# First batch of a gated-MLP attention kernel: f32 products and transpositions on TensorE in place of split halves and DMA transpositions

## Chip, core and metric

The kernel runs on one core of one Trainium2 chip. The metric is the device time of one launch in microseconds (us); before the change it is the median of three runs. PE is TensorE, DVE VectorE, ACT ScalarE, POOL GpSimd, SP the engine that issues all the DMAs here.

## What is computed

Eight batches of eight heads of causal attention with an added decay, and then a gated MLP per batch. Sequence 576, head width 64, model width 512, MLP width 1024.

```python
scores = scale * np.matmul(q, k.transpose(0, 1, 3, 2))
bias = -(cum[:, :, :, None] - cum[:, :, None, :])      # cum = cumsum(max(s, 0))
scores = np.where(causal, -1000000000.0, scores + np.minimum(bias, 0.0))
scores = scores - np.max(scores, axis=-1, keepdims=True)
attn = np.exp(scores)
attn = attn / (np.sum(attn, axis=-1, keepdims=True) + 1e-09)
x = np.matmul(attn, v)                                  # heads side by side: 576 x 512
h = np.maximum(x @ w_in, 0.0)
u, v = (h[..., :d_ff // 2], h[..., d_ff // 2:])
v_n = (v - mu) / np.sqrt(var + 1e-06)
v_s = np.einsum('ts,bsd->btd', w_spatial, v_n) + b_spatial[None, :, None]
out = (u * v_s) @ w_out
```

## The kernel before

Work is cut into 32 **pairs** of heads (four pairs make a batch) and eight MLPs. Where f32 accuracy is wanted, most operands are kept as two f16 halves, a high and a low one, and a product is two or three f16 matmuls; the three weights are split in this way once, at the start.

A pair p goes through these steps (names as the planner has them):

- `sc`: scores, in seven PSUM groups (`BANKS`). From pair 3 on (`NNAT = 3`) they come from two f16 matmuls (L463), whose operands ACT rounds (`h`, L413), POOL subtracts (`l`, L406) and four DMAs move into place. Pairs 0 to 2 take f32 q and k as they are loaded and one f32 matmul (L460), with the decay rows copied in by `nsel` (L304) and `ncum` (L308). A f32 matmul leaves two records in the trace.
- `red` (L469, DVE): mask and row maximum. `exp` (L487, ACT): exponential and row sum. `sum` (L492, L493, L497, DVE): the inverse of the sums.
- `hi` (L513, ACT) and `lo` (L515, DVE): the normalised weights as high and low halves, four instructions each per head, and one each for the two heads' last 64 rows (`thi`, `tlo`).
- `turn`, `tturn` (L522): three DMA transpositions per pair, issued by SP.
- `av` (L620, L627, PE): weights times V in three f16 products; V's halves come from `vh` (L585, ACT) and `vl` (L587, DVE), for two pairs at a time. `xh`, `xl` (L636, L640) split the result for the MLP.

An MLP runs `gate` (L670), `up` (L764), the spatial product `sp` (L779, L781, L782) and `dn` (L808) on PE, with ACT, DVE and POOL between them. The weights' conversion at the start is `wb`, `wq`, `wd`, `wh`, `wl` (L340 to L349, L320, L321) for each of twelve blocks, DVE in the main.

The order on every engine is made when the kernel is built: `Plan.order` walks through all steps with a guessed duration for each and takes, on each free engine, the ready step with the lowest place. The places come from the table of numbers `X`. On the chip each engine then works through its own list strictly in that order, and waits where an operand or a buffer isn't ready. PSUM has three banks each in `psS` and `psM` for scores and MLP products, one for `av` and one for the last rows.

Of the kernel before, what the change touches and what calls it, by code (L numbers as in the profile page):

```python
# [17 lines left out]
SV = 64.0  # L18
# [115 lines left out]
X = {"load": -5.2, "prep": -2.2, "vf": -0.5, "vc": 1.5, "red": 0.0, "exp": 0.092, "sum": -0.172, "hi": -0.219, "lo": -0.36, "turn": 0.06, "tsum": 0.528, "thi": 0.133, "tlo": 0.08, "tturn": 0.09, "av": 3.72, "av3": 5.635, "xh": 0.358, "xl": -0.701, "m0": 10.3, "span": 8.0, "mb0": -0.073, "mb1": 0.0, "n1": -25.0, "n2": 2.0, "l3": 0.5, "p3": 4.805, "vf0": 0.688, "vc0": 1.4, "vf1": 4.402, "vc1": 6.4, "fv": 1.483, "fvd": 1.2, "cv": 7.171, "cvd": 0.531, "fu": 4.5, "fud": 1.0, "cu": 9.0, "cud": 0.5, "wo": 10.6, "wod": 1.1, "sp": 11.0, "spd": 0.4, "sp4": 10.635, "bias": 0.2, "hv": 0.0, "bn": 0.01, "nm": 0.03, "vh": 0.04, "vl": 0.05, "uc": -0.671, "gm": 0.0, "gh": 0.01, "gl": 0.02, "oc": -0.113, "out": 0.01, "sc": 0.333, "sc0": 0.0, "up0": 0.0, "sp0": 0.0, "dn0": 0.0}  # L134


def mm(*cols):
    return sum(0.4167 * c + 3 for c in cols)
# [11 lines left out]
def attn_gated_mlp(ctx, tc, qkT, v, s, w_in, w_spT, b_sp, w_out, outT):  # L150
# [20 lines left out]
    NNAT = 3  # L171
# [25 lines left out]
    mhalf = cp.tile([P, 1], F32, name="mhalf")  # L197
    cc = cp.tile([NH, 3, S], F16, name="cc")
# [18 lines left out]
    def masks4():  # L217
# [5 lines left out]
        nc.gpsimd.memset(mhalf, -0.5)  # L223

    add("mb", POOL, 1700, -19, masks)
    add("mb4", POOL, 1200, -18, masks4)
# [61 lines left out]
    add("bp", POOL, 6000, X["bias"] + .1, lambda: bias_rows(1), need=["bf"])  # L288
# [4 lines left out]
    ntag = (("g1", "g2", 1, ["g1", "g2"]), ("xt1", "xt2", 2, ["xt"]), ("xt1", "xt2", 2, ["xt"]))  # L293
# [9 lines left out]
    def native_sel(p):  # L303
        [nc.vector.tensor_copy, nc.scalar.copy, nc.scalar.copy][p](  # L304
            raws[p, "q"][0:NH], sel[:, 2 * p:2 * p + 2].unsqueeze(2).to_broadcast([NH, 2, S]))

    def native_cum(p, j):
        [nc.vector.tensor_copy, nc.vector.tensor_copy, nc.scalar.copy][p](raws[p, "k"][0:NH, j], cst["cum"])  # L308

    for p in range(NNAT):  # L310
        at = (-27.0, X["n1"], X["n2"])[p]
        add(("nk", p), SYNC, 650, at, lambda p=p: native_load(p, "k"), take=ntag[p][3], move=(0, 1070))
        add(("nq", p), SYNC, 650, at + .1, lambda p=p: native_load(p, "q"), need=[("nk", p)], move=(0, 1070))
        add(("nsel", p), (DVE, ACT, ACT)[p], (700, 1150, 1150)[p], at + .2, lambda p=p: native_sel(p), need=[("nq", p)])
        for j in range(2):
            add(("ncum", p, j), (DVE, DVE, ACT)[p], (400, 400, 650)[p], at + .3 + .1 * j,
                lambda p=p, j=j: native_cum(p, j), need=[("nk", p), "cum"])
# [73 lines left out]
    BLK = (2, 0, 3, 6)  # L391
    pts = {}
# [32 lines left out]
    def attend(p):  # L425
# [98 lines left out]

        for b, (j, ics) in enumerate(BANKS):
# [45 lines left out]
    def values(hb):  # L571
        i = hb % 2

        def fetch():
            b, x = divmod(hb, 2)
            cols = slice(4 * D * x, 4 * D * x + 4 * D)
            raw = wk.tile([P, NC5, 4 * D], F32, tag="vraw", bufs=1, name=f"vraw{hb}")
# [5 lines left out]
        old = [("av", 2 * hb - 3)] if hb > 1 else []  # L583
        add(("vf", hb), SYNC, 1000, a0, fetch, take=["vraw"], move=(0, 1660))
# [13 lines left out]
    def output(p):  # L598
# [4 lines left out]
        def products():  # L603
            ph, pt4 = [pts.pop((p, j)) for j in range(2)], pts.pop((p, None))
            if pr == 0:
                xt[b] = (wk.tile([P, KC, S], F16, tag="xt1", bufs=2, name=f"xt1_{b}"),
                         wk.tile([P, KC, S], F16, tag="xt2", bufs=2, name=f"xt2_{b}"))
                avt[b] = psT.tile([P, 4, TAIL], F32, tag="T", name=f"avt{b}")
            av = avs[p] = psV.tile([P, 512], F32, tag="V", name=f"av{p}")
            for jc in range(NFULL):  # L610
                for n, (off, V) in enumerate(((0, V1), (0, V2), (10, V1))):
                    for q0 in ((max(jc, 1), 0) if jc == 0 else (jc,)):
                        for j in range(2):
# [4 lines left out]
                            else:  # L618
                                rhs, dst = ph[j][:, off + BLK[0]], av[o, 0:P]
                            nc.tensor.matmul(dst, V[i][:, jc, h + j], rhs, start=jc == n == 0 and q0 > 0,  # L620
                                             stop=jc == 3 and n == 2)
            t = avt[b][:, pr]
            for jc in range(NC5):
                for n, (off, V) in enumerate(((0, V1), (0, V2), (5, V1))):
# [267 lines left out]
```

## Time and profile before

| | |
|---|---|
| median of three runs | 677.1 us (675.7 to 677.91) |
| the profiled execution | 675.81 us, of which the span in the trace is 674.0 us |
| busy over the span | PE 593.3, DVE 570.7, ACT 508.8, POOL 137.0 us |
| mean granted PE clock | 0.959 of 2.4 GHz |

Busy PE means that a matmul was in flight. A share of the span is an average over a start in which PE has little to do and a long rest in which it has no pause, so the stretches are shown apart below. The granted clock is a share of full speed: 1.00 is 2.4 GHz, and a stretch between 0.5 and 1.0 was at 1.2 GHz for a part of it.

### The profile page before, as it was taken

What the parts mean: (1) busy time and instruction counts of PE and PEld (TensorE: products, weight loads), DVE (VectorE), ACT (ScalarE), POOL (GpSimd) and SP (SyncE); (2) the same over time, 40 slices, a digit from 0 to 9 for tenths busy, and PEclk for the clock granted to TensorE, in tenths of its full rate; (3) what the DMA queues carried; (4) which work ended last, traced back from release to release, by engine and by line L of the source; (5) the groups of instructions that cost most, each with busy time, mean ns of one, the idle gap of its engine ahead of it and who ended that gap; (6) DMA issues with size and microseconds to landing.
All of it is one profiled execution on the core that took longest, in us unless ns stands there. A gap on an engine that the chain in (4) does not pass through costs nothing. (4 is left out here: it accounts for less than half of the span.)

```text
span 674.0 us, 15717 instructions
## 1 busy us (share of the span) xinstructions
PE 593.3 (88%) x5696; PEld 408.7 (61%) x5696; DVE 570.7 (85%) x1544; ACT 508.8 (75%) x1319; POOL 137.0 (20%) x188
## 2 busy tenths in 40 slices
PE   2556446979998999999998999899999999999997
PEld 1232322757746775677656775677566765777675
DVE  6999999999799898989898989989888989892630
ACT  4868678796878788788968897879869887874422
POOL 9720221110312112311132021211231111000200
PEclk9886757989999999999999999999999999999999
DMA  8999999978997999879986999598967987564001
GB/s 249 290 216 237 142 205 222 211 195 160 172 240 151 178 216 241 158 148 239 203 195 147 220 186 236 136 202 194 244 164 129 217 183 130 92 117 131 1 13 70
DMA packets 245347, 119.28 MB, mean 177 GB/s; under 512 B 213864, under 2 KB 227350, under 8 KB 245271
## 3 DMA queue, kind: packets, MB, share of 16 engines
q1 hardware_dynamic: 245271, 118.30, 81.2%
q8 instruction: 44, 0.72, 0.4%
q14 instruction: 32, 0.26, 0.1%
HBM read 37.48 MB, written 9.66 MB: 70 GB/s over the span
## 5 line engine op out<-in xcount | busy, mean ns | idle before, releaser
L487 ACT ACTIVATE p<-psS,mx 128x128 f32<-128x128 f32 (+3 forms) x256 | 133.2, 526 | 38.3 <-DVE mx L469 37.5
L406 POOL TENSOR_TENSOR QB<-raw,KA 128x288 f16<-128x288 f32 x116 | 89.6, 802 | 299.8 <-ACT KA L413 299.7
L469 DVE CUSTOM_DVE_ANT_0 psS<-psS,mb 128x128 f32<-128x128 f32 (+3 forms) x288 | 134.5, 475 | 8.2 <-PE psS L463 2.8
L513 ACT ACTIVATE pb<-p,sm 128x384 f16<-128x384 f32 (+3 forms) x256 | 123.5, 552 | 22.3 <-issue 11.6
L515 DVE SCALAR_TENSOR_TENSOR pb<-p,sm,pb 128x384 f16<-128x384 f32 (+3 forms) x256 | 129.9, 556 | 5.2 <-ACT pb L513 3.9
L463 PE MATMUL psS<-KA,QA 128*128 128x128 f16 (+1 forms) x348 | 83.0, 313 | 32.6 <-ACT p L487 23.9
L764 PE MATMUL ups<-xt,win 128*128 128x288 f16 x768 | 102.4, 286 | 7.3 <-ACT u L769 7.2
L779 PE MATMUL sps<-ws,vn 128*128 128x288 f16 x768 | 105.5, 287 | 0.0
L808 PE MATMUL ops<-g,wo 128*128 128x288 f16 x768 | 101.5, 286 | 0.7 <-ACT ob L815 0.7
L670 PE MATMUL vps<-win,xt 128*128 128x512 f16 (+1 forms) x576 | 99.0, 348 | 0.1
L764 PEld LDWEIGHTS <-win 128*128 128x128 f16 x768 | 73.9, 98 | 33.0 <-issue 11.2
L808 PEld LDWEIGHTS <-wo 128*128 128x128 f16 x768 | 74.5, 98 | 25.0 <-issue 2.7
L463 PE MATMUL psS<-KB,QB 128*128 128x128 f16 (+1 forms) x348 | 89.3, 308 | 0.0
L779 PEld LDWEIGHTS <-vn 128*128 128x128 f16 x768 | 74.3, 98 | 24.2 <-issue 2.1
L670 PEld LDWEIGHTS <-xt 128*128 128x128 f16 (+1 forms) x576 | 47.8, 103 | 48.8 <-issue 7.1
L620 PE MATMUL av<-pT,V 128*64 128x128 f16 (+2 forms) x960 | 63.1, 285 | 8.0 <-DMA pT<-pb 5.5
L696 POOL TENSOR_TENSOR rs<-rs,mhalf 128x1 f32<-128x1 f32 x40 | 24.8, 619 | 199.4 <-DVE rs L692 175.0
L620 PEld LDWEIGHTS <-V 128*64 128x64 f16 x960 | 49.2, 115 | 26.4 <-issue 14.7
L463 PEld LDWEIGHTS <-QA 128*128 128x128 f16 x348 | 30.2, 102 | 37.2 <-issue 29.9
L487 ACT ACTIVATION_READ_ACCUMULATOR p<-psS,mx 128x1 f32 x256 | 51.5, 201 | 0.0
L460 PE MATMUL psS<-kraw,qraw 128*128 128x128 f32 (+5 forms) x72 | 23.5, 553 | 27.4 <-ACT p L487 14.0
L469 DVE DVE_READ_ACCUMULATOR2_ANT mx<- 128x1 f32 x320 | 45.6, 142 | 0.0
(80 smaller groups left out, 791.2 us busy)
## 6 DMA issues: line engine op xcount, KB each, us to landing
raw<-in_qkT_dram SPq DMA_DIRECT2D x29, 576.0 KB
out_dram<-ob SPq DMA_DIRECT2D x32, 288.0 KB
vraw<-in_v_dram SPq DMA_DIRECT2D x16, 512.0 KB
QA<-KA SPq DMA_DIRECT2D x29, 144.0 KB
KB<-KA SPq DMA_DIRECT2D x29, 144.0 KB
KB<-QB SPq DMA_DIRECT2D x29, 144.0 KB
QB<-KA SPq DMA_DIRECT2D x29, 144.0 KB
wst<-in_w_in_dram SPq DMA_DIRECT2D x8, 512.0 KB
```

What stands on the lines that cost most here:

```text
L406: nc.gpsimd.tensor_tensor(out=QB[i][:, j, cs], in0=raws[p][:, j, cs], in1=KA[i][:, j, cs], op=ALU.subtract)
L463: nc.tensor.matmul(ps[m, c0:c0 + w], U[i][:, g, q0:q0 + n], T[i][:, g, k0:k0 + w], start=st, stop=not st)
L469: nc.vector.tensor_tensor_reduce(out=ps[:, c0:c0 + w], in0=ps[:, c0:c0 + w], in1=mask, op0=ALU.add, op1=ALU.min, scale=-0.125, scalar=mx[: ...
L487: nc.scalar.activation(dst, ps[:, c0:c0 + w], AF.Exp, bias=mx[:, mcol:mcol + 1], scale=-1.0, accum_out=sm[:, col:col + 1])
L513: nc.scalar.activation(dst[:, off:off + w], src, AF.Copy, bias=0.0, scale=sc)
L515: nc.vector.scalar_tensor_tensor(out=dst[:, n + off:n + off + w], in0=src, scalar=sc, in1=dst[:, off:off + w], op0=ALU.mult, op1=ALU.subtract)
L620: nc.tensor.matmul(dst, V[i][:, jc, h + j], rhs, start=jc == n == 0 and q0 > 0, stop=jc == 3 and n == 2)
L670: nc.tensor.matmul(ps[m, 0:w], xx[:, c, t * P:t * P + (m.stop - m.start)], ww[:, c, NF + g * w:NF + g * w + w], start=c == n == 0, stop=c ...
L696: nc.gpsimd.tensor_tensor(out=rs, in0=rs, in1=mhalf, op=ALU.pow)
L764: nc.tensor.matmul(ps[:, 0:TH], ww[:, c, fs], xx[:, c, ts], start=n == 0, stop=n == 3 * KC - 1)
L779: nc.tensor.matmul(ps[:, 0:TH], vv[:, c, fs], ww[:, c, ts], start=n == 0, stop=False)
L808: nc.tensor.matmul(ps[:, 0:TH], ww[:, f, ms], gg[:, f, ts], start=n == 0, stop=n == 3 * FC - 1)
```

## The change

For the first batch (pairs 0 to 3, `NNV = 4`) three things change.

- Pair 3's scores are f32 products too (`NNAT = 4`): its `h`, `l` and four DMA moves go, `nsel` and `ncum` on ACT come.
- The weights aren't split and no DMA transposes them. POOL multiplies an identity matrix that holds 64 on its diagonal (`eye`) by the inverse sums, which gives a diagonal matrix per block of 128 rows (`dg`, 512 and 640 columns a pair). PE multiplies each of the 25 blocks of 128x128 exponentials of a pair by its diagonal in f32 (`tp`), which transposes and normalises it in one product; ACT copies the result from PSUM (`te`, eight copies a pair, f32).
- `av` takes these and V as it was loaded, one f32 product in place of three f16 ones, so `vh` and `vl` of the first two loads go.

The diagonals and the second load of V use the buffers `pb` that held the halves. All numbers in `X` are others too, so the order on every engine differs, in the later batches as well. At the start SP issues two blocks of `w_in` and a third k ahead of the first q, and DVE does the first block's `wb` ahead of `nsel` of pair 0.

```diff
-    NNAT = 3
+    NNAT = 4
+    NNV = 4
...
+        nc.gpsimd.memset(eye, 0.0)
+        nc.gpsimd.affine_select(out=eye, in_=eye, pattern=[[-1, P]], compare_op=ALU.not_equal, fill=SV, base=0,
+                                channel_multiplier=1)
...
+        def diagonals(j):
+            if j == 0:
+                cell["dg"] = wk.tile([P, 10, P], F32, tag="pb", bufs=room["pb"], name=f"dg{p}")
...
+            n = 4 + j
+            eng.tensor_tensor(out=cell["dg"][:, 4 * j:4 * j + n], in0=eye.unsqueeze(1).to_broadcast([P, n, P]),
+                              in1=cell["sm"][:, 4 * j:4 * j + n].unsqueeze(2).to_broadcast([P, n, P]), op=ALU.mult)
+
+        def transpose(j, k):
...
+            for x, n in enumerate(TB[j][k]):
...
+                nc.tensor.matmul(ps[:, P * x:P * x + P], src, cell["dg"][:, col], start=True, stop=True)
+
+        def keep(j, k):
...
+            src = cell["tp", j, k][:, 0:P * len(blocks)].rearrange("p (n q) -> p n q", q=P)
+            if EV[j][k] is ACT:
+                nc.scalar.copy(dst, src)
...
+            if p < NNV:
+                dg = DG[p]
+                add(("dg", p, j), dg, {POOL: 1450 + 350 * j, DVE: 700 + 130 * j}[dg], at + X["dg"], lambda j=j: diagonals(j),
+                    need=[("sum", p, j), "mb4"], take=["pb"] if j == 0 else (), give=["mx"] if j else ())
+                for k, blocks in enumerate(TB[j]):
...
+                    add(("tp", p, j, k), PE, mm(*[4 * P] * len(blocks)), at + X["tp"] + .01 * k,
+                        lambda j=j, k=k: transpose(j, k), need=[("dg", p, j)], take=[bk],
+                        give=(["p32"] + (["q32", "pb"] if j else [])) if last_k else ())
...
+        if 2 * hb + 1 < NNV:
+            return
         add(("vh", hb), ACT, 1160, a1, lambda: nc.scalar.activation(V1[i], vraws[hb], AF.Copy, bias=0.0, scale=SV),
...
-                for n, (off, V) in enumerate(((0, V1), (0, V2), (10, V1))):
+                for n, (off, V) in enumerate(vv):
...
+                            val = V[i][:, jc, h + j] if V else vraws[p // 2][:, jc, h + j]
+                            nc.tensor.matmul(dst, val, rhs, start=jc == n == 0 and q0 > 0,
+                                             stop=jc == 3 and n == len(vv) - 1)
```

On PE, between the scores of the first pair and those of the second, there stood nothing before (`psS_223` and `psS_231` are the first pair's, `psS_241` the second's):

```order
L460 MATMUL psS_217<-kraw_119,qraw_146 128x512
L460 MATMUL psS_223<-kraw_119,qraw_146 128x256
L460 MATMUL psS_223<-kraw_119,qraw_146 64x128 x2
L460 MATMUL psS_231<-kraw_119,qraw_146 64x512 x2
L460 MATMUL psS_241<-kraw_121,qraw_150 128x128
L460 MATMUL psS_241<-kraw_121,qraw_150 128x384
```

Now the transpositions of the first pair's first head stand there, and those of its second head (`tp_10` and on) before the second half of the second pair's scores:

```order
L470 MATMUL psS_242<-kraw_120,qraw_151 64x512 x2
L549 MATMUL tp_00_266<-dg_259,p_0_230 128x128 x4
L549 MATMUL tp_01_280<-dg_259,p_0_230 128x128 x4
L549 MATMUL tp_02_287<-dg_259,p_0_230 128x128 x2
L470 MATMUL psS_294<-kraw_122,qraw_154 128x128
L470 MATMUL psS_294<-kraw_122,qraw_154 128x384
L470 MATMUL psS_302<-kraw_122,qraw_154 128x512
L470 MATMUL psS_307<-kraw_122,qraw_154 128x256
L549 MATMUL tp_10_314<-dg_259,p_1_249 128x128 x4
```

So PE's list now holds, between two groups of scores, products that wait for POOL's diagonal of the pair before.

On DVE, around the inverse sums of the first pair's second head, the four low halves (`pb`) stood ahead of them before:

```order
L469 ISA mx_239 128x1
L515 SCALAR_TENSOR_TENSOR pb_258<-p_0_213,sm_186,pb_258 128x384
L515 SCALAR_TENSOR_TENSOR pb_258<-p_0_213,sm_186,pb_258 128x512
L515 SCALAR_TENSOR_TENSOR pb_258<-p_0_213,sm_186,pb_258 128x128
L515 SCALAR_TENSOR_TENSOR pb_258<-p_0_213,sm_186,pb_258 128x256
L497 TENSOR_TENSOR sm_186<-sm_186 128x1
L492 TENSOR_SCALAR sm_186<-sm_186 128x5
L493 RECIPROCAL sm_186<-sm_186 128x5
```

Now a piece of a weight's conversion (`wt`) stands there:

```order
L479 ISA psS_242,mx_196<-psS_242,mb,mx_196 128x512
L479 ISA mx_196 128x1
L355 SCALAR_TENSOR_TENSOR wt<-wst,wt 128x512
L346 TENSOR_SCALAR wt<-wst 128x512
L347 SCALAR_TENSOR_TENSOR wt<-wst,wt 128x512
L349 SCALAR_TENSOR_TENSOR wt<-wst,wt 128x512
L507 TENSOR_TENSOR sm_197<-sm_197 128x1
L502 TENSOR_SCALAR sm_197<-sm_197 128x5
L503 RECIPROCAL sm_197<-sm_197 128x5
```

The low halves of the first four pairs are gone from DVE's list, and the conversions have moved forward into their room.

On POOL, the low halves of q and k stood before, of pairs 3, 4, 5 and on:

```order
L282 TENSOR_TENSOR cst<-cst 1x576
L280 CAST cst<-cst 1x576
L406 TENSOR_TENSOR QB_82<-raw_136,KA_76 128x288 x4
L406 TENSOR_TENSOR QB_83<-raw_170,KA_77 128x288 x4
L406 TENSOR_TENSOR QB_84<-raw_312,KA_78 128x288 x4
```

Now only pair 4's come first, and the diagonals (`dg`) follow them:

```order
L265 TENSOR_TENSOR cc<-cst,cc 64x576
L416 TENSOR_TENSOR QB_83<-raw_163,KA_77 128x288 x4
L540 TENSOR_TENSOR dg_259<-eye,sm_197 128x512
L540 TENSOR_TENSOR dg_259<-eye,sm_197 128x640
L540 TENSOR_TENSOR dg_362<-eye,sm_293 128x512
L540 TENSOR_TENSOR dg_362<-eye,sm_293 128x640
L540 TENSOR_TENSOR dg_481<-eye,sm_407 128x512
```

Eight diagonals have come onto POOL, in the path from a pair's sums to its transposition.

## Rows read from the trace of the kernel before

**Rows 1.** Busy time by stretch: start:end, length, each engine (instructions), granted PE clock, DMA, GB/s

```profile
core 0: us, PE busy (x) PEld busy (x) DVE busy (x) ACT busy (x) POOL busy (x), PEclk, DMA share, GB/s
0.00:11.80 11.80, 0.00 (x0) 0.00 (x1) 7.01 (x7) 3.72 (x4) 10.67 (x22) 1.00 0.83 221
11.80:107.90 96.10, 51.01 (x384) 27.72 (x384) 92.43 (x235) 75.14 (x193) 29.54 (x31) 0.75 0.98 225
107.90:147.55 39.65, 34.87 (x322) 22.04 (x321) 37.71 (x98) 31.54 (x74) 8.75 (x13) 0.93 0.93 197
147.55:602.00 454.45, 439.33 (x4379) 308.66 (x4377) 407.56 (x1142) 372.48 (x991) 84.40 (x118) 1.00 0.87 183
602.00:674.00 72.00, 68.11 (x617) 50.30 (x614) 25.96 (x65) 25.93 (x62) 3.68 (x5) 1.00 0.21 57
```

**Rows 2.** PE's timeline: start, length, line, output and inputs, shape, count

```profile
107.92 13.78 PE L670 MATMUL vps<-win,xt 128*128 128x512 f16 x72
...
147.55 2.43 PE L779 MATMUL sps<-ws,vn 128*128 128x288 f16 x12
```

**Rows 3.** Waits of PE from 11.8 to 107.9: who for whom, total us, times, longest

```profile
PE psS L463 <- ACT p L487: 16.8, 4, 7.7
PE psS L460 <- ACT p L487: 14.0, 2, 8.5
...
PE av L620 <- DMA pT<-pb: 5.0, 1, 5.0
```

**Rows 4.** DVE's L515 alone, from 0 to 92 us: busy time and count

```profile
0.00:92.00 92.00, 20.22 (x36) 0.79 0.99 227
```

**Rows 5.** Groups of instructions on DVE from 0 to 106: count, busy us, mean ns

```profile
L587 DVE SCALAR_TENSOR_TENSOR V<-vraw,V 128x1280 f16<-128x1280 f32 x3 | 4.7, 1577 | 1.3 <-ACT V L585 1.3
```

**Rows 6.** Timelines of DVE and POOL: start, length, engine, line, shape, count

```profile
23.38 3.30 DVE L515 SCALAR_TENSOR_TENSOR pb<-p,sm,pb 128x384 f16<-128x384 f32 x4
...
24.59 6.11 POOL L406 TENSOR_TENSOR QB<-raw,KA 128x288 f16<-128x288 f32 x8
...
26.60 0.68 DVE L497 TENSOR_TENSOR sm<-sm 128x1 f32<-128x1 f32 x1
...
39.62 4.40 POOL L406 TENSOR_TENSOR QB<-raw,KA 128x288 f16<-128x288 f32 x4 [8.92 <-ACT KA L413]
...
100.33 0.15 DVE L497 TENSOR_TENSOR sm<-sm 128x1 f32<-128x1 f32 x1
...
102.54 1.93 DVE L515 SCALAR_TENSOR_TENSOR pb<-p,sm,pb 128x384 f16<-128x384 f32 x4
```

**Rows 7.** PE's f32 scores (L460) alone, in a stretch of unbroken products

```profile
19.63:22.43 2.80, 2.80 (x13) 1.00 1.04 284
```

**Rows 8.** PE alone by stretches of 20 us: length, busy (count), granted clock, DMA

```profile
40.00:60.00 20.00, 7.58 (x74) 0.67 1.02 228
...
100.00:120.00 20.00, 14.74 (x64) 0.83 0.98 220
120.00:140.00 20.00, 19.88 (x228) 1.00 0.98 212
```

**Rows 9.** PE's timeline around the first `av`

```profile
39.21 1.83 PE L620 MATMUL av<-pT,V 128*64 128x384 f16 x30
...
41.45 0.70 PE L460 MATMUL psS<-kraw,qraw 128*128 128x256 f32 x2
```

**Rows 10.** Groups of instructions on ACT from 0 to 107.9

```profile
L513 ACT ACTIVATE pb<-p,sm 128x384 f16<-128x384 f32 (+3 forms) x44 | 21.1, 555 | 1.7 <-DVE sm L493 1.7
...
L513 ACT ACTIVATE pb<-q,sm 128x640 f16<-128x640 f32 x5 | 4.1, 815 | 0.0
L636 ACT ACTIVATE xt<-av 128x512 f16<-128x512 f32 x4 | 2.4, 592 | 0.0
```

**Rows 11.** Waits of PE from 147.55 to the end

```profile
PE ups L764 <- ACT u L769: 7.2, 5, 1.4
PE psS L463 <- ACT p L487: 5.9, 16, 0.6
```

More of the change, by code (lines that the diff above doesn't have):

```diff
@@ L287, in attn_gated_mlp @@
     add("bf", SYNC, 650, X["bias"], lambda: bias_rows(0), need=["s0"], move=(0, 100))
[L288 removed]
+    add("bp", POOL, 6000, X["bias"] + .1, lambda: bias_rows(1), need=["bf"] + ([("dg", NNV - 3, 1)] if NNV > 2 else []))
     add("bx", SYNC, 1950, X["bias"] + .2, lambda: bias_rows(2), need=["bp"], move=(1300, 100))
@@ L391, in attn_gated_mlp @@
     BLK = (2, 0, 3, 6)
+    TB = (((0, 1, 2, 3), (4, 5, 6, 7), (8, 9)), ((0, 1, 2, 3), (4, 5, 6, 7), (8, 9), (10, 11, 12, 13), (14,)))
+    TBANK = ("psS", "psM")
+    EV = ((ACT, ACT, ACT), (ACT, ACT, ACT, ACT, ACT))
+    DG = (POOL,) * NNV
     pts = {}
@@ L548, in attend @@
                 need=[("exp", p, j, ic) for ic in range(4)] + ([("tsum", p)] if j else []))
+            if p < NNV:
[3 more added lines that the diff above has]
+                for k, blocks in enumerate(TB[j]):
+                    bk, last_k = TBANK[k % len(TBANK)], k == len(TB[j]) - 1
+                    w = P * len(blocks)
+                    add(("tp", p, j, k), PE, mm(*[4 * P] * len(blocks)), at + X["tp"] + .01 * k,
+                        lambda j=j, k=k: transpose(j, k), need=[("dg", p, j)], take=[bk],
+                        give=(["p32"] + (["q32", "pb"] if j else [])) if last_k else ())
+                    ev = EV[j][k]
+                    add(("te", p, j, k), ev, dve(w) if ev is DVE else act(w), at + X["te"] + .01 * k,
+                        lambda j=j, k=k: keep(j, k), need=[("tp", p, j, k)],
+                        take=["pT"] if k == 0 else ["pT4"] if j and k == 3 else (), give=[bk])
+                if j == 0:
+                    continue
+                add(("tsum", p), DVE, 75, t5 + X["tsum"], tail_sum, need=[("exp", p, 1, 4), ("exp", p, 1, 9)])
+                return
             for n, ic in enumerate((2, 3, 0, 1)):
@@ L642, in output @@
         at = 2 * p + (X["av"] if p > 3 else X["av3"])
-        add(("av", p), PE, 2000, at, products, need=[("turn", p, 0), ("turn", p, 1), ("tturn", p), ("vl", p // 2)],
-            take=["psV"] + (["psT", "xt"] if pr == 0 else []), give=["pT", "pT", "pT4"])
+        need = [("turn", p, 0), ("turn", p, 1), ("tturn", p), ("vl", p // 2)] if p >= NNV else \
+            [("vf", p // 2)] + [("te", p, j, k) for j in range(2) for k in range(len(TB[j]))]
+        used = ["pT", "pT", "pT4"] + ([("pb" if p // 2 == 1 else "vraw")] if p < NNV and p % 2 else [])
+        add(("av", p), PE, 2000 if p >= NNV else 2600, at, products, need=need,
+            take=["psV"] + (["psT", "xt"] if pr == 0 else []), give=used)
         for k in range(2 if pr == 3 else 1):
```

56 lines of the change are left out of this document (40 added, 16 removed).

## Prediction

> **What bounds the kernel now.** I read the busy time by stretch first [rows 1]. From 147.55 us to the end PE is busy for 507.4 of 526.5 us: there PE is the bound, and its list of work after 147.55 isn't touched in kind, only reordered. Before 107.9 it is another kernel: in 96.1 us PE is busy for 51.0 at a mean granted clock of 0.75, while DVE is busy for 92.4, that is 96%. From 107.9 to 147.55 both are at their limit, DVE with 37.7 and PE with 34.9 of 39.65 us. The two marks are PE's first MLP product (L670, 107.92) and its first spatial product (L779, 147.55) [rows 2]. I then read who PE waits for in the first of these stretches [rows 3]: mostly for ACT's exponentials, which free the PSUM banks, and once 5.0 us for a DMA transposition. ACT itself isn't full there (75.1 of 96.1); its exponentials wait for the row maxima in DVE's list. So DVE sets the pace of the start, and the mark to argue with is the first spatial product: the same steps stand ahead of it in both kernels, but for those that the change drops or adds and some two microseconds of pair 6's low halves. What it moves, the end moves, as long as PE stays full behind it.
>
> **The change part by part.**
>
> *DVE, removed.* The low halves of pairs 0 to 3 are nine instructions of L515 for each pair, 36; exactly these ran up to 92 us: 20.2 us [rows 4]. Two low halves of V at 1.58 us: 3.2 us [rows 5]. Together 23.4 us off the engine that sets the pace. Nothing new comes onto DVE.
>
> *POOL, added, and what it costs DVE.* Eight diagonals, 4 x (512 + 640) columns. Nearest is L406, 288 columns, two operands: 6.11 / 8 = 0.76 us in one group and 4.40 / 4 = 1.10 in another [rows 6]; scaled by columns that is 12.2 to 17.6 us in all, 1.4 to 2.4 each, on an engine that is idle for most of the stretch. But the same rows show what such an instruction does to DVE: beside the 6.11 us of L406, four L515 took 3.30 in place of 1.93 and a single L497 0.68 in place of 0.15, so DVE lost 1.9 us, 0.31 per us of POOL. For 12.2 us that is 3.8; pair 3's four L406, which go, give back half of 1.9, so 2.9 us net (0, if the diagonals fall beside row maxima, to 5.5 for 17.6 us of POOL). DVE's account: 23.4 - 2.9 = 20.5 us less, so the mark could come at 127.0.
>
> *PE, added.* A f32 product's price: 2.80 us without a pause at full clock [rows 7] hold 1600 columns (128, 384, 512, 256, 128 and half of 384, the half being one of its two records), 1.75 ns a column. A 128-column block is then 0.224 us, 100 blocks 22.4 us. Pair 3's scores have 3200 such columns, 5.6 us, and cost half of that as two f16 products: +2.8. `av` with its tail took 41.45 - 39.21 = 2.24 us [rows 9] for three passes; a f32 product streams four times, 4/3 of that, +0.75 each, +3.0 for four. In all 28.2 us. PE's busy 85.9 up to the mark [rows 1] become 114.1, and PE can start about one microsecond later than 11.8: two weight blocks go ahead of the first q on SP and a conversion step ahead of `nsel` on DVE (I take 12.8). Without any wait the mark stands at 126.9. That is the same as DVE's account, by chance, and it is no floor: of the 51.0 us in the cold stretch up to 12.8 (a quarter) are the lower clock's, and the granted clock [rows 8] rises with PE's share, 0.67 where it was busy for 7.6 of 20 us, 0.83 at 14.7, 1.00 at 19.9.
>
> *ACT.* It loses 32 + 4 high halves, 32 x 0.555 + 4 x 0.815 = 21.0 us, and gains 32 copies out of PSUM, each no longer than L636's 0.592 [rows 10], at most 18.9. Pair 3's `nsel` takes the place of `h` at the same size, and two `ncum` copies add about 1.3 us by L636's rate. V's two high halves go too. ACT ends no fuller than before; it gets tighter only because the stretch gets shorter.
>
> *SP and DMA.* Twelve transpositions and four moves go. DMA is busy 0.98 of this stretch [rows 1], but PE waited 5.0 us for it in all [rows 3]; I count nothing, between 0 and a gain of 5.0, because DVE is behind these waits as well.
>
> *The new waits.* PE's list now has `tp` between two groups of scores; each waits for DVE's sum and POOL's diagonal, and behind it in PE's list stand the next pair's scores, for which DVE's row maxima wait in turn. That loop (scores, maximum, exponential, sum, diagonal, block) is covered by what PE does between: 2.8 to 3.4 us of blocks or scores of the other head, sometimes an `av`. A diagonal of 1.4 to 2.4 us and the sum are new in it, the two passes over the halves and 5 us of transposition are out. DVE has some conversion steps to fill a hole, but these run out. The same PSUM banks also serve 32 more groups. With both engines at 127 and neither able to be full all the time, I take 6 us of added waiting; none is the one end, and 20.5, all of the gain, the other.
>
> *The later batches.* The order differs there too. PE's idle time behind the mark is 19.0 us, 7.2 of it for `ucopy` and 5.9 for exponentials [rows 11], so no order can gain more than that; I count 0, with 3 us either way.
>
> *Sum.* 20.5 - 6 = 14.5 us off the mark, all of it carried to the end by a full PE. Against the profiled execution: 675.8 - 14.5 = 661.3, span 659.5. The median shown was 1.3 us above that execution: 677.1 - 14.5 = **662.6**.
>
> **The rivals.**
>
> *A. DVE's time is what counts (the forecast).* Waiting of 0 to 13 us: a gain of 7.5 to 20.5, 656.6 to 669.6, likeliest 662.6. For it: DVE's 96% with PE and ACT below 80%.
>
> *B. PE becomes the bound of the start.* 28.2 us of PE work come into a stretch where PE had 45 us of waits, most of them for banks that ACT frees, and the list is strict. If the mean clock stays near 0.75 and 13 to 20 us of waits remain beside the 114.1, the gain is 0.5 to 7.5: 669.6 to 676.6. Against it: those waits were for exponentials held up in DVE's list.
>
> *C. Slower: the blocks don't lift the clock.* Ahead of the first MLP product PE has 4 x 5.6 (scores) + 2.8 (pair 4) + 22.4 + 4 x 3.0 = 59.6 us of work at full clock. At the lower level, 1.2 GHz, it is 119.2, and with the start at 12.8 the first MLP product comes at 132.0 in place of 107.9, 24 us later: 701. The point from which it is slower is a mean clock of 59.6 / (107.9 - 12.8) = 0.63 over this stretch with no wait at all. The trace speaks against it: the f32 scores ran at 1.00 [rows 7], and only stretches with PE idle more than half of the time show 0.67 [rows 8]. The Trainium skill, "TensorE: Matmul & The Clock Gate", "Part 4: PE-mode transpose", says that the clock does not rise for products in the engine's transpose mode. By that rule, if it held for a plain f32 product against a diagonal, the time would be that 701; no row here shows such a product.
>
> *D. More than DVE's account.* The clock's share on PE comes back, the 5 us of DMA wait goes, and later stalls shrink: 20.5 to 28 less, 649 to 656.6.
>
> *E. It doesn't do what it says.* The start is shorter, but the later order gives it back, with `ucopy` and bank waits growing by as much: 677, 2 us either way. Against it: PE is 97% busy there before [rows 1], and its work stays the same.
>
> **How the numbers follow.** A 0.66, B 0.15, C 0.06, D 0.07, E 0.06. The prediction is A's 662.6. The range 651 to 676 takes in A, nearly all of B and most of D and leaves out C, most of E and D's end, about 0.13. A measurement of this kernel can tell 0.3%, 2 us, from no change. Faster by more: A, D and most of B (0.13), 0.86. Within: a rest of B and half of E, 0.05. Slower: C and the rest of E, 0.09.
>
> **What would show it.** Right: L515 and the V halves absent up to pair 4; DVE still above 90% busy before the first spatial product, which stands near 133; the first MLP product near 93; a block every 0.22 us at a granted clock above 0.85 in the start; the span behind the first spatial product still about 526 us. Wrong in the waits: DVE below 85% there with PE waiting for POOL's diagonals. Wrong towards B: PE above 90% busy before 93. Wrong towards C: blocks 0.43 us apart and a clock below 0.63. Wrong towards E: the first spatial product early and the stretch behind it longer than 530. The diagonals show their price at once, and DVE's single-column instructions beside them show what they cost it.

## The result, and the profile after

The changed kernel takes 649.0 us (median, 646.81 to 653.91), the kernel before 677.37 on the same chip: a ratio of 0.9595, 95% interval 0.9538 to 0.9652. The prediction was 662.6 with a range of 651 to 676, so the gain is 28.4 us where 14.5 were forecast, and the time lies just below the range. The profiled execution took 649.36 us, with a span of 647.1 against 674.0.

The busy time by stretch of the changed kernel, cut at its own marks (columns as in [rows 1]):

```profile
0.00:13.90 13.90, 0.00 (x0) 0.01 (x1) 10.13 (x11) 4.25 (x5) 12.71 (x25) 1.00 0.85 202
13.90:80.94 67.04, 64.20 (x481) 46.67 (x481) 58.14 (x166) 56.71 (x156) 26.65 (x26) 0.97 0.54 165
80.94:132.88 51.94, 40.93 (x353) 24.61 (x350) 47.98 (x130) 44.13 (x107) 15.93 (x21) 0.90 0.90 207
132.88:575.00 442.12, 435.64 (x4374) 306.64 (x4373) 391.80 (x1138) 372.31 (x989) 81.20 (x118) 1.00 0.90 188
575.00:647.10 72.10, 68.43 (x617) 50.19 (x615) 26.40 (x66) 25.64 (x60) 3.69 (x5) 0.99 0.22 59
```

The second row answers to the second of [rows 1]. There PE was busy for 51.0 of 96.1 us at a clock of 0.75; now it is busy for 64.2 of 67.0 at 0.97, and DVE, at 96% before, is at 87%. The third row is where PE now waits: 11.0 us of 51.9.

The marks in PE's timeline of the changed kernel (start, length, line, output and inputs): its first MLP product, its first spatial product, and the first spatial product of the second batch:

```profile
80.94 1.90 PE L743 MATMUL vps<-win,xt 128*128 128x512 f16 x8
...
132.88 1.63 PE L852 MATMUL sps<-ws,vn 128*128 128x288 f16 x12
...
199.67 1.52 PE L852 MATMUL sps<-ws,vn 128*128 128x288 f16 x11
```

Before, the first two stood at 107.92 and 147.55 [rows 2], and the third here:

```profile
219.87 1.64 PE L779 MATMUL sps<-ws,vn 128*128 128x288 f16 x12
```

The stretch between the second and the third mark, and the one behind the third, first of before:

```profile
147.55:219.87 72.32, 68.94 (x646) 47.38 (x644) 65.50 (x178) 57.44 (x153) 12.47 (x17) 0.99 0.87 185
...
219.87:674.00 454.13, 438.51 (x4350) 311.58 (x4348) 368.03 (x1029) 340.98 (x900) 75.60 (x106) 1.00 0.76 163
```

and the same two of after:

```profile
132.88:199.67 66.79, 66.21 (x641) 46.89 (x640) 60.06 (x171) 55.93 (x147) 11.13 (x17) 1.00 0.92 195
...
199.67:647.10 447.43, 437.85 (x4350) 309.94 (x4348) 358.13 (x1032) 342.02 (x903) 73.76 (x106) 1.00 0.79 166
```

So the 26.9 us of the span are 14.7 up to the first spatial product (147.55 to 132.88), 5.5 between it and that of the second batch (72.32 to 66.79), and 6.7 behind (454.1 to 447.4). The forecast put 14.5 up to the first mark and nothing behind it. Behind it PE's idle time fell from 19.0 us [rows 1] to 10.2 (the last two rows of the first table: 514.2 - 435.64 - 68.43), and its busy time by 3.4.

### The profile page after: what moved, and what is told of

Same layout as the page of the kernel before. It is cut to its first block, busy times and chain, and to the rows that moved or that the text cites. A ratio compares the mean times of both kernels' runs of the same rounds, so it can differ in the third digit from the quotient of the medians.

```text
span 647.1 us, 15913 instructions
## 1 busy us (share of the span) xinstructions
PE 609.2 (94%) x5816; PEld 428.1 (66%) x5816; DVE 534.4 (83%) x1506; ACT 503.0 (78%) x1315; POOL 140.2 (22%) x194
## 5 line engine op out<-in xcount | busy, mean ns | idle before, releaser
L497 ACT ACTIVATE p<-psS,mx 128x128 f32<-128x128 f32 (+3 forms) x256 | 133.5, 528 | 29.4 <-DVE mx L479 22.1
L416 POOL TENSOR_TENSOR QB<-raw,KA 128x288 f16<-128x288 f32 x112 | 82.5, 767 | 248.9 <-ACT KA L423 235.9
L525 DVE SCALAR_TENSOR_TENSOR pb<-p,sm,pb 128x384 f16<-128x384 f32 x224 | 110.6, 546 | 8.4 <-ACT pb L523 8.1
L523 ACT ACTIVATE pb<-p,sm 128x384 f16<-128x384 f32 x224 | 108.3, 554 | 8.4 <-issue 3.2
L743 PE MATMUL vps<-win,xt 128*128 128x512 f16 (+1 forms) x576 | 97.4, 344 | 1.3 <-DVE xt L710 0.9
L881 PEld LDWEIGHTS <-wo 128*128 128x128 f16 x768 | 74.1, 98 | 22.4 <-issue 0.4
L473 PE MATMUL psS<-KA,QA 128*128 128x128 f16 (+1 forms) x336 | 77.6, 308 | 9.8 <-ACT p L497 5.4
L473 PE MATMUL psS<-KB,QB 128*128 128x128 f16 (+1 forms) x336 | 84.4, 303 | 0.0
L689 PE MATMUL av<-pT,V 128*64 128x128 f16 (+2 forms) x840 | 53.1, 279 | 0.4 <-DMA pT<-pb 0.3
L689 PEld LDWEIGHTS <-V 128*64 128x64 f16 x840 | 41.0, 112 | 15.9 <-issue 5.3
L473 PEld LDWEIGHTS <-QA 128*128 128x128 f16 x336 | 27.7, 102 | 25.4 <-issue 15.7
L860 DVE SCALAR_TENSOR_TENSOR g<-sps,u 128x288 f32<-128x288 f32 x64 | 28.9, 453 | 13.2 <-PE sps L855 12.8
```

The costliest lines, as they stand in the source:

```text
L416: nc.gpsimd.tensor_tensor(out=QB[i][:, j, cs], in0=raws[p][:, j, cs], in1=KA[i][:, j, cs], op=ALU.subtract)
L473: nc.tensor.matmul(ps[m, c0:c0 + w], U[i][:, g, q0:q0 + n], T[i][:, g, k0:k0 + w], start=st, stop=not st)
L497: nc.scalar.activation(dst, ps[:, c0:c0 + w], AF.Exp, bias=mx[:, mcol:mcol + 1], scale=-1.0, accum_out=sm[:, col:col + 1])
L523: nc.scalar.activation(dst[:, off:off + w], src, AF.Copy, bias=0.0, scale=sc)
L525: nc.vector.scalar_tensor_tensor(out=dst[:, n + off:n + off + w], in0=src, scalar=sc, in1=dst[:, off:off + w], op0=ALU.mult, op1=ALU.subtract)
L689: nc.tensor.matmul(dst, val, rhs, start=jc == n == 0 and q0 > 0, stop=jc == 3 and n == len(vv) - 1)
```

## The experiments

For all kernels I use the first spatial product of the second batch ("the mark" below). The same 4350 PE products stand behind it in before, after, e6, e7 and e11, 4356 in e2; in the others the planner put 57 to 73 products more ahead of it, so there only PE's idle time behind the mark is compared, not the length. The times are medians, with the ratio to the kernel before (676.7 to 676.9 in these jobs) and its interval; the other columns are of the profiled execution, idle time "ahead" counted from the span's start. e6 and e11 keep the order of the changed kernel on every engine; in the others the planner knows other numbers, steps or durations and makes another order, so that their times hold an effect of the order besides that of the work.

| kernel | us | ratio, 95% | mark at | PE idle ahead | PE idle behind | PE busy in all |
|---|---|---|---|---|---|---|
| before | 677.4 | | 219.9 | 65.0 | 15.7 | 593.3 |
| after | 649.0 | 0.9595 (0.9538 to 0.9652) | 199.7 | 28.3 | 9.6 | 609.2 |
| e1_numbers_alone | 678.8 | 1.0036 (1.0008 to 1.0065) | 230.7 | 69.1 | 11.3 | 597.2 |
| e2_old_numbers | 673.4 | 0.9945 (0.9922 to 0.9968) | 216.0 | 40.3 | 17.0 | 615.6 |
| e3_old_numbers_late | 666.7 | 0.9849 (0.9817 to 0.9881) | 209.4 | 33.2 | 18.7 | 611.8 |
| e4_no_blocks | 675.6 | 0.9974 (0.9951 to 0.9997) | 229.4 | 61.2 | 11.9 | 602.9 |
| e5_dve_work_back | 679.3 | 1.004 (1.0018 to 1.0061) | 238.0 | 51.5 | 10.3 | 620.8 |
| e6_blocks_twice | 669.8 | 0.9903 (0.9879 to 0.9926) | 224.0 | 29.4 | 6.5 | 631.6 |
| e7_new_numbers_late | 674.5 | 0.9965 (0.9938 to 0.9991) | 223.1 | 67.6 | 8.9 | 592.4 |
| e8_six_pairs | 660.5 | 0.9763 (0.973 to 0.9796) | 212.8 | 27.6 | 10.6 | 619.7 |
| e9_mlp_old_late | 670.5 | 0.9913 (0.9886 to 0.9939) | 211.4 | 35.4 | 18.0 | 620.4 |
| e10_attention_old_late | 664.1 | 0.9832 (0.9786 to 0.9878) | 207.5 | 32.7 | 18.1 | 611.5 |
| e11_diagonals_twice | 654.4 | 0.9659 (0.9625 to 0.9693) | 207.4 | 34.8 | 8.0 | 610.2 |
| e12_diagonals_dve | 664.4 | 0.9812 (0.9779 to 0.9845) | 215.3 | 37.5 | 10.4 | 615.5 |

The profiled executions of e5 and e9 were 5.5 us above their medians, that of e7 3.7 below, so the idle times of these three are the less certain ones.

### The places without the blocks, and the blocks without the places

e1 is the kernel before with the changed kernel's table; X_BEFORE and X_AFTER stand for the two tables.

```diff
-X = X_BEFORE
+X = X_AFTER
```

> The kernel before with the new numbers in X and nothing else of the change. Theory 1 (the 12.2 us gained behind the first spatial product come from the new order in the later batches): that stretch falls from 526.5 to 514 to 518 us here too, with the first spatial product near 147.5, so 662 to 670. Theory 2 (they come from the state in which the shorter start leaves the engines, DVE and ACT further ahead): the stretch stays at 524 to 529 and the time at 674 to 682.

e2 is the changed kernel with the table of before, except the numbers of the steps that the change itself makes or shifts (`bias`, the loads of pair 3's k and of the first two V, `n1` to `n3`, `dg`, `tp`, `te`).

```diff
-X = X_AFTER
+X = {**X_AFTER, **X_BEFORE, **{k: X_AFTER[k] for k in ("bias", "l3", "p3", "vf0", "vc0", "vf1", "vc1", "n1", "n2", "n3")}}
```

> The changed kernel with the old numbers in X, but for the ten places of the first loads, which it needs (bias, l3, p3, vf0, vc0, vf1, vc1, n1 to n3) and the keys that only it has. Theory 1: first spatial product at 133 to 138, the stretch behind it near 526, 659 to 665. Theory 2: first spatial product the same, the stretch behind it near 514, 647 to 653.

The table alone costs 1.9 us (678.75 against 676.88), the blocks alone bring 3.5 (673.37), both together 28. Neither is worth anything much without the other. In e2, DVE's busy time up to the first spatial product falls by 21.7 us (137.16 to 115.42), about the account of the prediction, yet that product comes only 7.3 us earlier (140.21 for 147.55): DVE's idle time ahead of it rose by 14.4. Up to the mark in the second batch it is 20.5 us of work (202.65 to 182.16), 3.9 us of time and 16.6 of waits. e2 up to its first spatial product, PE's start in it, and then PE's longest waits up to the mark (who for whom, total us, times, longest), without those for the first loads:

```profile
0.00:140.21 140.21, 105.26 (x816) 72.13 (x816) 115.42 (x294) 103.46 (x261) 55.27 (x69) 0.93 0.65 171
...
13.90:102.33 88.43, 71.42 (x493) 50.19 (x494) 71.00 (x193) 68.63 (x182) 33.89 (x34) 0.90 0.59 166
```

```profile
PE psS L473 <- ACT p L497: 7.9, 7, 2.4
PE av L689 <- DVE xt L710: 5.6, 1, 5.6
PE tp L549 <- POOL dg L540: 3.4, 4, 1.6
PE psS L470 <- ACT p L497: 3.2, 1, 3.2
```

An `av` waits for DVE's split of x (`xl`), scores wait for exponentials, and blocks for diagonals. In span terms, e2 lies 25.9 us behind the changed kernel: 12.0 of PE's idle time ahead of the mark, 7.4 behind it, and 6.4 more busy time, at a lower clock in the start (0.90 to 102 us against 0.97 to 81).

e4 takes the blocks out of the changed kernel and leaves its table:

```diff
-    NNV = 4
+    NNV = 0
```

> The changed kernel with NNV = 0: pair 3's scores in f32 and all the new numbers stay, but weights and V of all pairs are split into halves and transposed by DMA as before. The forecast's account (DVE gets 23.4 us back, POOL gives 2.9): the first spatial product 14 to 21 us later than 132.9, at 147 to 154. With theory 1 the stretch behind it stays at 514 to 518: 662 to 672. With theory 2 it goes back to 526: 674 to 680.

It takes 675.6: with the new table the blocks are worth 26.6 us. Its waits of PE, over the whole span, are those of [rows 3] again, for exponentials and now also for the split of x:

```profile
PE psS L473 <- ACT p L497: 13.3, 8, 2.9
PE psS L470 <- ACT p L497: 10.9, 5, 7.2
PE av L689 <- DVE xt L710: 7.1, 3, 3.2
PE vps L743 <- DVE xt L710: 5.7, 1, 5.7
```

DVE has 204.8 us of work ahead of e4's mark, 204.4 in e1, 202.7 in before, and 176.3 in after (e1 and e4 have some 70 products more ahead of it). As long as that work is there, neither table helps.

Of the two theories in these texts and in e3's below, e1 and e4 have the times of the second, and e2 and e3 came out slower than either theory had it. Both took it that the start takes about the same time in either order, and it does not. So what lies behind the start is split below at the mark of the second batch, and compared by PE's idle time.

### Where the gain behind the start comes from

e3 is the changed kernel, whose later batches (pairs from 8 on, MLPs from the second on) take the old places; e7 is the kernel before, whose later batches take the new ones. X0 is the kernel's own table, X1 the other's. In e3:

```diff
     def mlp(b):
+        X = X1 if b >= 1 else X0
...
     def attend(p):
+        X = X1 if p >= 8 else X0
```

and the same line in `prepare`, `values` and `output`. In e7, `thi` of pair 8 was set to -1.8, besides.

> The changed kernel with its own numbers for pairs 0 to 7 and the first MLP, and the old numbers for pairs 8 to 31 and MLPs 1 to 7. Theory 1: first spatial product unchanged at 133, the stretch behind it back at 523 to 527, 657 to 661. Theory 2: unchanged, 647 to 652.

> The kernel before with the new numbers for pairs 8 to 31 and MLPs 1 to 7 only (one place of pair 8 bridged), the start's numbers as before. If the later order alone is worth 7 us, as the stretch behind the second MLP's first spatial product says (454.1 before, 446.9 with the new numbers alone): that stretch 446 to 449 and 668 to 672, unless the seam between the two orders loses it again. If the later order helps only behind the new start: 675 to 679.

These two make a square with before and after. PE's idle time behind the mark is 15.7 us (before) and 17.0 (e2) with the old places, 8.9 (e7) and 9.6 (after) with the new ones, with or without the blocks, and with the same number of products behind the mark. So the 6.7 us behind the mark are the order's, not the blocks'. e2 and then e7 behind their marks:

```profile
216.00:673.00 457.00, 439.92 (x4356) 311.75 (x4352) 368.69 (x1029) 342.33 (x903) 75.75 (x106) 1.00 0.74 161
...
223.06:668.80 445.74, 436.90 (x4350) 309.03 (x4348) 356.89 (x1027) 340.53 (x900) 73.17 (x106) 1.00 0.79 167
```

In medians, e3 is 17.7 us slower than the changed kernel (17.0 without its slowest execution); of the 16.5 in its profile, 9.1 are idle time behind the mark, 4.8 idle time ahead of it and 2.6 busy time. e7 is 2.2 us faster than the kernel before, between the two cases of its text, and less than the 6.8 us of idle time that went in its profile (its mark comes 3.2 us later than before's, and its profiled execution lies below its median). So the order's share in the idle time is shown, and what it is worth without the new start is less.

The waits of PE behind the mark in the kernel before, from 219.87 on:

```profile
PE ups L764 <- ACT u L769: 5.7, 4, 1.4
PE psS L463 <- ACT p L487: 5.3, 14, 0.6
```

and in the changed kernel, from 199.67 on:

```profile
PE ups L837 <- ACT u L842: 3.0, 4, 1.1
PE sps L854 <- DMA vx<-tl: 1.6, 3, 1.0
PE psS L473 <- ACT q L497: 0.7, 1, 0.7
```

Fourteen short waits for exponentials, 5.3 us, have become one of 0.7; those for the copies of u fell from 5.7 to 3.0. They are the greater part of the 7.2 + 5.9 us of [rows 11], in the 19.0 us that the prediction named as the most that an order could gain, and then counted at nothing.

DVE's busy time behind the mark fell as well, from 368.0 to 358.1 us for about the same instructions, and this goes with the late places too: it is 356.9 in e7 and 368.7 in e2. Taking each instruction's time over the median of its form, DVE lost about 16 us there beside POOL's L406 in the kernel before, and about 8 beside the same step (L416) in the changed one.

e9 and e10 split the new places: in e9 only the MLPs (the line in `mlp`), in e10 only attention (the other four) go back to the old ones.

> The changed kernel, whose MLPs from the second on take the places of the kernel before (among them gate's evictions, the statistics of vn, the copies of u, and the weights of the spatial product); attention keeps the new places throughout. Seven kernels with new late places needed 443.6 to 447.4 us behind the first spatial product of MLP 1, three with old ones 454.2 to 457.0. If the MLP's places make the difference: 452 to 457 behind that mark and 655 to 660 in all. If the places of attention make it (waits of PE's scores for exponentials): 444 to 448 and 649, 2 us either way. If it takes both together: in between, 650 to 654.

> The counterpart: the pairs of the third batch and on (pair 8 on) take the places of the kernel before, the MLPs keep the new ones. If the MLP's places make the 7 us: 444 to 448 us behind the first spatial product of MLP 1, and 649, 2 us either way. If attention's make it: 452 to 457, and 655 to 660 in all. If old and new places only don't suit each other: longer than with either set, above 460.

A correction to the figures in these two texts: of the kernels counted there as short behind the mark, e1, e4, e5 and e8 have up to 72 products more ahead of it; the idle times in the table are what can be compared, and they divide in the same way (6.5 to 11.9 us with new late places, 15.7 to 18.7 with old). With half of the places old, it is 18.0 (e9) and 18.1 (e10): each half alone loses all of it in these executions. Both times lie above every case of their texts, but for the last one of e10, which gives no time. PE's longest wait behind the mark, in e9 and then in e10:

```profile
PE psS L475 <- ACT p L499: 13.0, 5, 2.6
```

```profile
PE psS L477 <- ACT p L501: 10.9, 5, 3.3
```

So neither the MLP's places nor attention's hold the gain; they fit each other. DVE's busy time behind the mark is 368.4 us in e9 and 353.4 in e10, so that it goes with the MLP's places, and by itself it does not free PE. Which of the numbers matter within them stays open.

### What bounds the new start

e5 puts DVE work back: for each of the first four pairs nine instructions with two operands in SBUF, of the sizes of the nine low halves, at the places of `lo`, into a buffer that nobody reads.

```diff
+        def again(w):
...
+                for n, w in enumerate((384, 512, 128, 256) + ((640,) if j else ())):
+                    add(("again", p, j, n), DVE, dve(w), at + X["lo"] + .01 * n, lambda w=w: again(w),
+                        need=[("sum", p, j), "mb", "mb4"])
```

> The changed kernel, with DVE given nine further instructions for each of pairs 0 to 3, of the shapes of the low halves that went (two SBUF operands, 3200 columns a pair, results unused), 19 us in all. If DVE's time is still what counts at the start, the spatial product of the second MLP comes 16 to 20 us later than 199.7 and the time is 664 to 669. If PE has become the bound there (it is busy for 64.2 of 67.0 us before the first MLP product), DVE's idle 13 us before the first spatial product absorb most of it: 654 to 659.

e6 does each of the 100 blocks twice.

```diff
-                nc.tensor.matmul(ps[:, P * x:P * x + P], src, cell["dg"][:, col], start=True, stop=True)
+                for _ in range(2):
+                    nc.tensor.matmul(ps[:, P * x:P * x + P], src, cell["dg"][:, col], start=True, stop=True)
```

> The changed kernel with every transposition block computed twice into the same place, 25.5 us more on PE (22.4 by start-to-start) with the same order. If PE is the bound of the start now: 18 to 24 us more, 667 to 673. If DVE is: 5 to 12 more, 654 to 661.

The first stretch up to the first MLP product, in e5 and then in e6, and e6 from there to its first spatial product:

```profile
13.90:107.05 93.15, 73.46 (x481) 52.23 (x481) 83.86 (x195) 57.16 (x150) 32.59 (x30) 0.89 0.39 113
```

```profile
13.90:102.61 88.71, 86.19 (x681) 68.87 (x681) 57.68 (x166) 58.84 (x157) 26.29 (x26) 0.98 0.40 124
...
102.61:157.24 54.63, 41.94 (x353) 24.84 (x350) 48.40 (x131) 43.66 (x107) 15.91 (x21) 0.88 0.95 201
```

Both are paid in full. e6 adds 22.4 us to PE's busy time and takes 20.8 us longer; in its start PE is busy for 86.2 of 88.7 us. Up to the first spatial product DVE's busy time in e6 is what it is in the changed kernel, 116.2 us in all (57.7 and 48.4 in these two stretches, 58.1 and 48.0 there), and yet that product comes 24.4 us later (157.24 for 132.88): DVE has 41.0 us to spare there and catches nothing up. e5 takes 30.3 us longer, more than either case of its text. The inserted instructions were to be 19 us and took 25.9; DVE's busy time in all rose by 29.3 (534.4 to 563.7). PE waited for it, and the clock in the start fell from 0.97 to 0.89; e5's order is another one too, so the 30.3 aren't the work's alone. So in the new start PE is the bound, and DVE has no room either: no work was moved from a full engine to an idle one for free.

e8 gives blocks to pairs 4 and 5 as well.

```diff
-    NNV = 4
+    NNV = 6
```

> The changed kernel with NNV = 6: pairs 4 and 5 also go through f32 blocks and f32 V instead of halves and DMA transpositions, 2 x (5.6 + 0.75) = 12.7 us more on PE and about 11 less on DVE. If PE is full behind the first MLP product, the time rises by 8 to 13: 657 to 662. If DVE still sets the pace there, it falls by 3 to 10: 639 to 646.

It is 11.5 us slower than the changed kernel (660.5). The stretch of e8 between its first MLP product and its first spatial product:

```profile
88.18:133.14 44.96, 44.40 (x378) 31.48 (x376) 38.69 (x95) 34.94 (x91) 20.66 (x24) 1.00 0.55 143
```

The 11 us of PE's idle time of the changed kernel there are gone, at a clock of 1.00, DVE has 9 us less to do, and it is slower all the same. PE's busy time in all rose by 10.5 us, and the idle time came back elsewhere: ahead of the mark it is 27.6 us, against 28.3. DVE's busy time in all fell by 2.2 us only, where about 11 were expected; why stays open. In the order that the planner made for it, blocks for two more pairs cost PE their time and gained nothing.

### What the diagonals cost

e11 computes each diagonal twice on POOL, e12 once on DVE.

```diff
+            for _ in range(2):
-            eng.tensor_tensor(out=cell["dg"][:, 4 * j:4 * j + n], in0=eye.unsqueeze(1).to_broadcast([P, n, P]),
...
+                eng.tensor_tensor(out=cell["dg"][:, 4 * j:4 * j + n], in0=eye.unsqueeze(1).to_broadcast([P, n, P]),
...
```

> The changed kernel with every diagonal computed twice on GpSimd: 9.5 us more of POOL, in the same places, and each transposition waits 1.0 to 1.3 us longer for its diagonal. The prediction's price (DVE loses 0.31 us per us of POOL) gives DVE 2.9 us more. The price that the changed kernel's own rows gave (1.5 us lost beside 9.5) gives 1.5. If neither that nor the later diagonal costs anything, 649, 2 us either way; if contention alone counts, 650 to 653; if the diagonal is in a closed loop (scores, maximum, sum, diagonal, block), each of the eight delays everything by its own length: 9.5 us, 657 to 660.

```diff
-    DG = (POOL,) * NNV
+    DG = (DVE,) * NNV
```

> The changed kernel with the diagonals on DVE in place of POOL. By the four low halves of one head (1280 columns in 1.93 us, 1.5 ns a column) eight diagonals of 512 and 640 columns are 6.9 us of DVE. If DVE sets the pace as the prediction has it: 5 to 7 us later less the 1.5 us that POOL costs it now, 652 to 656. If, as with the nine instructions a pair put back, the clock on PE falls with it (30 us for 19): 1.6 for each us, 9 to 11 more, 657 to 661. If PE alone is the bound of the new start: 649, 2 us either way.

The eight diagonals of the changed kernel (count, busy us, mean ns, idle time before), and one of them:

```profile
L540 POOL TENSOR_TENSOR dg<-eye,sm 128x512 f32<-128x512 f32 (+1 forms) x8 | 9.5, 1182 | 34.3 <-DVE sm L503 29.0 <-ACT pN_t L564 5.3
```

```profile
23.15 1.04 POOL L540 TENSOR_TENSOR dg<-eye,sm 128x512 f32<-128x512 f32 x1 [1.48 <-DVE sm L503]
```

They take 9.5 us in all, not 12.2 to 17.6: 1.04 us for 512 columns and 1.26 for 640, so scaling L406's 288 columns was too dear. The Trainium skill, "GPSIMD Engine Reference", "3.1 Elementwise — side-by-side cycle accounting", gives about 2.6 cycles for an element of a two-operand `tensor_tensor`, at 1.2 GHz an estimate of 1.11 and 1.39 us, and the rows come out a little under it. The DVE conversion beside the first (L355) took 1.17 us, where the mean of its twelve is 0.80. Taking each DVE instruction's time over the median of its form, DVE lost 1.5 us beside them, 0.16 per us of POOL, in place of the 0.31 that I read from two places. In e11 it is 4.1 us beside 20.3, 0.20 per us. e11 costs 5.4 us (654.4), and its mark comes 7.7 later, of which DVE's busy time has 3.9 (176.3 to 180.3). It lies between contention alone (650 to 653) and a closed loop (657 to 660): PE's waits for diagonals rose from 2.7 us in two places to 3.9 in four, so a later diagonal is waited for in some of its eight places, not in all.

In e12 the diagonals, on DVE, took

```profile
L540 DVE TENSOR_TENSOR dg<-eye,sm 128x512 f32<-128x512 f32 (+1 forms) x8 | 6.9, 866 | 0.3
```

as expected, and the kernel 664.4, 15.4 us more than with POOL. That is above every case: DVE's busy time rose by 11.0 (534.4 to 545.5). Beside the 6.9 for the diagonals, L416's products on POOL now fell beside more of DVE's work, which lost about 6 us up to the mark beside them (under 2 in the changed kernel). PE's busy time rose by 6.3. The order there is another one too, since the planner knows another duration, so the 15.4 aren't DVE's price alone. Of the two, POOL is the better place for the diagonals: DVE loses 1.5 us to them there, and 6.9 if it does them itself.

## Why the prediction was wrong, point by point

**The reading of the bound: right for the kernel before, in part for the changed one.** e1 and e4, which leave DVE its work, stay within 2 us of the kernel before, with either table. But less work for DVE alone was not enough: in e2 it has 21.7 us less up to the first spatial product, and that comes 7.3 us earlier. And in the changed kernel DVE no longer sets the pace alone, as e6 shows.

**DVE's account: right.** Up to the first spatial product DVE's busy time fell from 137.2 to 116.2 us, 20.9 less, where 20.5 were forecast. The low halves alone, up to the second mark, first in before and then in after:

```profile
0.00:219.87 219.87, 51.71 (x94) 0.88 0.93 207
```

```profile
0.00:199.67 199.67, 29.45 (x56) 0.97 0.78 189
```

are 22.3 us less, for 38 instructions; 23.4 were forecast for 36 and two halves of V, which gave 3.2 more. **The contention term in it had the wrong sign.** I set 2.9 us net against DVE. Taking each instruction's time over the median of its form, DVE lost about 6.5 us beside L406 up to the first mark in the kernel before (I had seen 1.9), in the changed one 1.5 beside the diagonals, under 1 beside L416 and about 2 more than before beside the set-up of masks and decay rows. The single-column sums show it best, up to the second mark, in before (count, busy us, mean ns):

```profile
L492 DVE TENSOR_SCALAR sm<-sm 128x4 f32<-128x4 f32 (+1 forms) x21 | 6.0, 284 | 0.3
...
L497 DVE TENSOR_TENSOR sm<-sm 128x1 f32<-128x1 f32 x10 | 2.9, 293 | 1.6 <-ACT q L487 1.6
```

and in after:

```profile
L502 DVE TENSOR_SCALAR sm<-sm 128x4 f32<-128x4 f32 (+1 forms) x21 | 3.5, 167 | 0.5
...
L507 DVE TENSOR_TENSOR sm<-sm 128x1 f32<-128x1 f32 x10 | 1.5, 153 | 0.1
```

Same instructions, 3.9 us less: before, eight of the 31 fell beside L406 and took 0.58 us on the mean, in the changed kernel one fell beside L416. Some two row maxima and a piece of a weight more, which the new order puts ahead of the mark, hid this in the sum: the account came out right with two errors in it.

**The added waiting: right in number, for this order alone and in part by luck.** DVE's idle time up to the first mark rose from 10.4 to 16.6 us, 6.2 where 6 were taken, and the mark came at 132.88 where 133 was forecast. e2 shows that the 6 are no property of the change: with the old table the same blocks bring 14.4 us of it. I estimated a wait from the loop and never asked whose order it was. e6 shows that DVE's account plus a wait isn't what holds this mark in the changed kernel: with DVE's work the same, PE's moves it. DVE was busy for 87% of the time up to it, between the 90% that I had named as the sign of being right and the 85% of being wrong in the waits, and PE waited for diagonals for only 2.7 us.

**PE's account: right in its size, and its clock term in the wrong place.** The four pairs' new products, up to the first MLP product (count, busy us, mean ns):

```profile
L549 PE MATMUL tp<-dg,p 128*128 128x128 f32 x160 | 21.1, 291 | 2.7 <-POOL dg L540 2.7
L689 PE MATMUL av<-pN,vraw 128*64 128x384 f32 (+2 forms) x80 | 9.5, 383 | 0.0
L549 PE MATMUL tp<-dg,q 128*128 128x128 f32 x40 | 5.1, 275 | 0.0
L697 PE MATMUL avt<-pN_t,vraw 128*64 128x64 f32 x80 | 3.0, 222 | 0.0
```

The `av` are 12.5 us (12.0 forecast), the blocks 26.2 (22.4, at full clock), and PE started at 13.9 (12.8 taken). PE's busy time up to the first spatial product rose by 19.2 us (85.9 to 105.1), not by 28.2: some 9 us came back, of the 12.8 at the low clock that the prediction had counted and left to rival D, while the clock of the start rose from 0.75 to 0.97. (In all, PE's busy time rose by 15.9; the rest is the 3.4 less behind that product.) So PE's account without any wait, 119.0 us with its start, ended ahead of DVE's, 126.6 with the idle time of before.

**The first MLP product near 93: wrong.** It came at 80.94. PE was 96% busy there, the sign that the prediction had kept for rival B, at a time that B excluded because it had left the clock at 0.75. The gain of 12 us over the forecast did not last to the next mark: from 80.94 to 132.88 PE waited 11.0 us, 4.8 of them for exponentials and 3.4 for a load of decay rows.

**The later batches: the step that failed.** The prediction said of the order that it "differs there too", that PE's idle time behind the mark was 19.0 us, and counted 0, with 3 us either way. It was 12.2: 8.9 of the 19.0 us of idle time, and 3.4 of busy time, which the prediction had taken for the same. With 0 in this term the sum gives 662.6; with 12.2 it gives 650.4, and the median is 649.0. Of the 12.2, the 6.7 behind the second batch's mark are shown to be the order's (before, e2, e7, after). The 5.5 us in the second batch, where PE's waits fell from 3.4 to 0.6 us and its busy time by 2.7, were not tried by themselves.

**The rivals.** A's number held up to the first mark, its mechanism in part, and its time didn't. D has the right time, at the end of its range, by the clock's share and smaller later stalls; of its third reason, the 5.0 us for a DMA transposition went, and 3.4 for a load of decay rows came. B is refuted as a price, but e6 shows that its bound is real: PE is now the limit of the start. C is refuted: the clock rose. PE's timeline at the first two groups of blocks, and then the granted clock in these stretches:

```profile
24.25 3.90 PE L549 MATMUL tp<-dg,p 128*128 128x128 f32 x20 [2.40 <-POOL dg L540]
...
30.37 2.39 PE L549 MATMUL tp<-dg,p 128*128 128x128 f32 x20
```

```profile
24.25:27.94 3.69, 3.69 (x20) 0.61 1.03 257
30.37:32.60 2.23, 2.23 (x21) 1.00 0.42 130
```

The first ten blocks, behind a wait of 2.4 us, took 3.7 us at a mean of 0.61, so mostly at 1.2 GHz; the second ten took 2.2 us at 2.4 GHz, 0.22 us each. The rule that the Trainium skill states in "TensorE: Matmul & The Clock Gate", "Part 4: PE-mode transpose", of the engine's transpose mode, that the clock does not rise with it, does not hold for these plain f32 products against a diagonal. E is refuted: the stretch behind the first mark became shorter, not longer.

## What to carry to other kernels

A change that comes with a new order is one change, not two: here the blocks alone bring 3.5 us, the order alone costs 1.9, both together 28, so idle time of the bound engine behind the edit belongs into the sum with a share of its own when its order is redone (8.9 of 19.0 us here). Work moved from a full engine to one that idles for it can cost less than its sum: on PE some 9 of 28.2 us came back while the clock of the start rose from 0.75 to 0.97. Two pairs further on it paid no more (e8), though PE idled there too, so idle time in the stretch is not enough of a reason. An account that ends at the right mark does not show that its engine holds the mark; work added to the other engine does (e6). Before pricing what a new instruction on GpSimd costs VectorE, count what the old ones cost over the whole stretch, not at the two places that show it.

## What the runs showed of the hardware

- A f32 product of a 128x128 block against a diagonal, which transposes and scales it, took 0.22 us at full clock, and the clock was 0.97 over a start that holds 100 of them.
- GpSimd multiplied two f32 operands of 512 columns, both broadcast, in 1.04 us and of 640 in 1.26, against 0.76 to 1.10 for 288 columns of L406 in [rows 6]. Beside these products VectorE lost 0.16 to 0.20 us per us; in the kernel before, eight of the 31 sums of four, five and one columns ahead of the second batch's mark fell beside L406 and took 0.58 us on the mean, the other 23 took 0.18.
- Four pairs' DVE work put back in another form (e5) took 25.9 us where it was to take 19, and in that kernel TensorE's granted clock in the start was 0.89 in place of 0.97.
- The same VectorE work behind the second batch's mark took 368.0 us in one order and 358.1 in another; beside GpSimd's 288-column subtractions it lost about 16 us in the first and about 8 in the second.
